# All of w_mod and wq read by rows behind the first K tile, the last wo rows read behind the last V tile, three unread products before the last layer

## The chip, the cores and the metric

One NeuronCore of a Trainium2 chip runs the whole program. The metric is the device time of one execution in microseconds (us). TensorE (PE) multiplies matrices into PSUM, VectorE (DVE) and ScalarE (ACT) do elementwise work, SyncE (SP) issues nearly all transfers (DMAs), which then run on 16 DMA engines in the order of issue. All data are 32-bit floats.

## The reference

A transformer block for one decoded token of 8 sequences, with adaptive layer norm:

```
mod = silu(c) @ w_mod                       # [8, 6*512], split into sa, ca, ga, sb, cb, gb
h = layernorm(x) * (1 + ca) + sa
q = h @ wq                                  # 32 heads of 128
p = softmax(q . k_cache[last 2048] / sqrt(128))   # 8 K/V heads, 4 query heads share one
x = x + ga * ((p . v_cache[last 2048]) @ wo)
h = layernorm(x) * (1 + cb) + sb
x = x + gb * (relu(h @ w1 + b1)**2 @ w2 + b2)
```

K and V of the window are 64 MiB each; w_mod is 6 MiB, wq and wo 8 MiB each, w1 and w2 3.5 MiB each.

## The kernel before, in words

**Buffers.** SBUF holds two "big" slots of 4 MiB and five "small" slots of 2 MiB (line 79). A K tile, which is half the batch of one K/V head, takes a big slot (16 of them, K0 to K15); a V tile, which is two sequences of one head, takes a small one (32, V0 to V31). Weights pass through the same slots.

**Order of the transfers.** One list, `loads` (lines 144 to 152), is the order in which SP issues every load; `pump` issues the next one as soon as a slot of its size is free in the program's order, and SP then waits until the slot's last reader is done. The list begins K0, columns of w_mod for sa and ca ("modA", 2 MiB), half of wq in two pieces, K1, the other half of wq, K2. Then comes a K tile followed by two V tiles, with a quarter of wo (2 MiB, a pair of heads) ahead of every eighth V tile: the last quarter stands ahead of V28. Behind V31 come the other four sixths of w_mod ("modB", 4 MiB, two DMAs), b1 and b2, w1 in two DMAs, w2 in four.

**Order of the compute.** It is written out by hand: PE executes in program order. The beginning makes mod's first two parts, the layer norm, and q (`project_q`, heads 0 to 3 first, 4 to 7 at step 4), with the first transposes of K0 in between. The main loop (line 501) has 38 steps, two steps to a K tile. A step transposes half a K tile on PE (line 231), which ACT and DVE copy out of PSUM (line 233), multiplies queries with it (line 359), and runs the V product `weighted` (line 451) five steps behind. A head's softmax (`soft_a` to `soft_d`), the gathering of its output (`gather`, line 475) and its product with wo (`project_o`, line 490) are placed at fixed steps. In step 33 stand, one behind the other, gather of head 6, the rest of head 7's softmax, the V product with V28, and `project_o(6)`; V29, V30 and V31 follow in steps 34 to 36, then in step 37 gather and `project_o(7)`.

**The end.** `at_i` copies the attention output out of PSUM (lines 540 and 541), `modulation` makes ga, sb, cb (line 543, 16 products of 384 columns) and gb (line 564, 16 of 128 columns), line 552 spreads at_i over partitions, x1 and its layer norm follow, then w1 (line 594), the squared ReLU (602 to 606), one product that nothing reads (line 611), w2 (line 614), and the output.

Of the kernel before, what the change touches and what calls it, by code (L numbers as in the profile page):

```python
# [20 lines left out]
def tile_adaln_cached_attention_mlp(  # L21
# [65 lines left out]
    def size_of(key):  # L87
        return "big" if key[0] in ("K", "modB") or key == ("wo", HKV // 2 - 1) else "small"

    def load(key):  # L90
        kind, i = key
        if kind == "b":
            nc.sync.dma_start(b1_in, b1.rearrange("(g n) -> g n", g=NQ))
            nc.sync.dma_start(b2_in, b2.rearrange("(g n) -> g n", g=NQ))
            return
        held[key] = free[size_of(key)].pop(0)
        t = slots[size_of(key)][held[key]]
        if kind in "KV":
# [7 lines left out]
            nc.sync.dma_start(t, v)  # L106
            return
        if kind == "wo":

            r = 2 * REP * DH  # L110
            v = wo[i * r : (i + 1) * r, :].rearrange("(h p i) n -> p h (i n)", p=P, i=4)
        elif kind == "modA":
            v = w_mod[:, : 2 * D].rearrange(r_kc, p=P)
        elif kind == "modB":
            v = w_mod.rearrange(r_kc, p=P)
            for lo, hi in ((2, 5), (5, 6)):
                nc.sync.dma_start(
                    t[:, NQ * D * (lo - 2) : NQ * D * (hi - 2)].rearrange("p (a n) -> p a n", a=NQ),
                    v[:, :, D * lo : D * hi],
                )  # L120
            return
        elif kind == "wq":
            r, half = divmod(i, 2)
            v = wq[:, 2048 * r : 2048 * r + 2048].rearrange(r_kc, p=P)[:, 2 * half : 2 * half + 2]
        elif kind == "w1":
            v = w1.rearrange(r_kc, p=P)[:, 2 * i : 2 * i + 2]
        else:
            v = w2.rearrange("(p c) n -> p c n", p=P)
            for lo, hi in ((0, 8),) if i == 0 else ((8, 12), (12, 13), (13, 14)):
                o = lo - 8 * i  # L130
                n = hi - lo
                nc.sync.dma_start(
                    t[:, D * o : D * (o + n)].rearrange("p (c n) -> p c n", n=D), v[:, lo:hi, :]
                )
            return
        a, n = v.shape[1:]
        nc.sync.dma_start(t[:, : a * n].rearrange("p (a n) -> p a n", n=n), v)

    def slot(key, n):

        t = slots[size_of(key)][held[key]]
# [18 lines left out]
    def done(*keys):  # L160
        for k in keys:
            free[size_of(k)].append(held.pop(k))
        pump()
# [58 lines left out]
    def transposes(q, g, e):  # L222

        k = slot(("K", q), DH)
        if e == 0:
            KTS[q, g] = ktp.tile([P, 4, 16, 32], F32, name="kT")
        t = KTS[q, g]
        for a in range(2):
            p = ps_kt.tile([P, 4, P], F32, name="kt_ps")
            for i in range(4):  # L230
                nc.tensor.transpose(p[:, i, :], k[:, 32 * e + 8 * g + 4 * a + i, :], ident)  # L231
# [21 lines left out]
    def modulation(wms, nq):  # L253

        pm = ps_m.tile([P, 512], F32, name="m_ps", tag="m_ps")
        for kc in range(NQ):
            wv = wms[kc].rearrange("p (m q n) -> p m q n", m=nq, q=NQ)
            for q in range(NQ):
                nc.tensor.matmul(
                    pm[32 * q : 32 * q + 32, : nq * P].rearrange("p (m n) -> p m n", m=nq),  # L260
                    cT[:, kc, :],
                    wv[:, :, q, :],
                    start=(kc == 0),
                    stop=(kc == NQ - 1),
                )
        return pm[:, : nq * P].rearrange("p (m n) -> p m n", m=nq)

# [8 lines left out]

    EARLY = [(0, 0), (0, 1), (0, 2)]
    transposes(0, 0, 0)
    transposes(0, 0, 1)
# [4 lines left out]
    modA = consts.tile([P, 2, P], F32, name="modA")  # L284
    m = slot(("modA", 0), 2 * D)
    pm = modulation([m[:, kc, :] for kc in range(NQ)], 2)
    done(("modA", 0))
    nc.vector.tensor_copy(modA[:, 0, :], pm[:, 0, :])
    nc.vector.tensor_scalar(modA[:, 1, :], pm[:, 1, :], 1.0, None, op0=ALU.add)
# [11 lines left out]
    h = work.tile([P, P], F32, name="h_sb", tag="one_h_sb", bufs=1)  # L301
    nc.vector.scalar_tensor_tensor(h, x_in, nmean, modA[:, 1, :], op0=ALU.add, op1=ALU.mult)
    transposes(0, 1, 0)
# [5 lines left out]
    nc.vector.scalar_tensor_tensor(h, h, rstd, modA[:, 0, :], op0=ALU.mult, op1=ALU.add)  # L309
    hT = consts.tile([P, NQ, 32], F32, name="h1T")  # L310
    to_columns(h, hT)
    transposes(0, 1, 1)

    def project_q(r, between=()):
        pq = ps_m.tile([P, 512], F32, name="m_ps", tag="m_ps")
        for kc in range(NQ):
            w = slot(("wq", 2 * r + kc // 2), 2048)
            for g in range(4):
                nc.tensor.matmul(  # L319
                    pq[32 * g : 32 * g + 32, :],  # L320
                    hT[:, kc, :],
                    w[:, kc % 2, 512 * g : 512 * g + 512],
                    start=(kc == 0),
                    stop=(kc == NQ - 1),
                )
            if kc % 2:
                done(("wq", 2 * r + kc // 2))
                if between:
                    transposes(*between[kc // 2])
        qs = work.tile([P, 512], F32, name="qs", tag="a", bufs=1)  # L330
        nc.scalar.copy(qs, pq)
# [8 lines left out]
    project_q(0, ((0, 2, 0), (0, 2, 1)))  # L340
# [101 lines left out]
    def weighted(n, h):  # L442
# [6 lines left out]
        for g in range(4):  # L449
            j = 8 * g + 4 * h  # L450
# [35 lines left out]
    def project_o(hk):  # L486

        w = slot(("wo", hk // 2), D)
# [8 lines left out]
        if hk % 2:  # L497
            done(("wo", hk // 2))


    for s in range(N + PV_LAG + 1):
# [4 lines left out]
        if s == C:  # L506
            project_q(1)
# [18 lines left out]
        if s < N:  # L526
            scores(q, 2 * h)
        if i == 0 and soft:
            soft_b(g - 1)
# [12 lines left out]
    m = slot(("modB", 0), 3 * D)  # L542
    pm = modulation([m[:, kc, :] for kc in range(NQ)], 3)
    ga = consts.tile([P, P], F32, name="ga")
    mul = consts.tile([P, P], F32, name="mul")
    add = consts.tile([P, P], F32, name="add")
    nc.scalar.copy(ga, pm[:, 0, :])
    nc.vector.tensor_scalar(mul, pm[:, 2, :], 1.0, lo, op0=ALU.add, op1=ALU.mult)
    nc.vector.tensor_scalar(add, pm[:, 1, :], hi, None, op0=ALU.mult)
# [13 lines left out]
    m = slot(("modB", 0), D)  # L563
    pmC = modulation([m[:, 3 * NQ + kc, :] for kc in range(NQ)], 1)
# [11 lines left out]
    modC = consts.tile([P, P], F32, name="modC")  # L576
    nc.scalar.copy(modC, pmC[:, 0, :])
# [3 lines left out]
    w1t = [slot(("w1", k), F) for k in range(2)]  # L581
    w2t = [slot(("w2", k), D) for k in range(2)]
# [28 lines left out]
    nc.tensor.matmul(spin_ps, ident, ident[:, None, :].to_broadcast([P, 4, P]), start=True, stop=True)  # L611
    for f in range(FC):
        for q in range(NQ):
# [3 lines left out]
                w2t[f // 8][:, f % 8, q * P : (q + 1) * P],  # L617
# [43 lines left out]
```

## Time and profile before

| | |
|---|---|
| median of 3 runs | 397.95 us (397.9 to 398.24) |
| the profiled execution | 399.03 us |
| its span, first to last instruction | 397.2 us |
| PE busy | 327.0 us, 82% of the span |
| DVE, ACT busy | 179.1 us, 97.0 us |
| moved by DMA | 165.22 MB, mean 416 GB/s |
| mean granted PE clock | 0.974 |

The profile is of one execution. Its views used below: the page (busy shares in 40 equal slices; queues), the timeline (each row: start, duration, engine, line, what it writes and reads, how often; in brackets how long the engine had been idle and what ended that), the DMA view (us from issue to landing) and windows (busy time of each engine in a stretch, then the granted PE clock, the busy share of the DMA engines, GB/s). Durations on PE are modelled: rows of one engine overlap a little.

### The profile page before, as it was taken

The numbers are of one execution on the slowest core, as the hardware profiler recorded it, in microseconds if no ns is written. First come the engines' busy times: TensorE is split into PE (matmuls) and PEld (weight loads), VectorE is DVE, ScalarE is ACT, GpSimd is POOL, SyncE is SP. The second block draws the span as 40 slices with busy tenths as digits, with TensorE's granted clock in tenths as the row PEclk, the third lists the DMA queues.
The fourth block names the chain that finished last, engine by engine and source line by source line (L and its number), as shares of the span: only waits on it lengthen the run. The fifth ranks groups of instructions, "written<-read, shape, count | busy, mean of one in ns | idle before, by whom it ended". The sixth has DMA issues, their size and how long they took to land.

```text
span 397.2 us, 6042 instructions
## 1 busy us (share of the span) xinstructions
PE 327.0 (82%) x2574; PEld 165.4 (42%) x2574; DVE 179.1 (45%) x417; ACT 97.0 (24%) x169; POOL 2.4 (1%) x12
## 2 busy tenths in 40 slices
PE   0477979796989968999869898998978789979574
PEld 0343535443444534444434444544444344533134
DVE  6142323553454435545623455555535364456320
ACT  1132224221222213123212232223122222230010
POOL 2000000000000000000000000000000000000000
PEclk9999999999899989999998999999999899989998
DMA  8999999999999999999999999999999999999992
GB/s 333 408 439 411 435 426 449 404 445 407 437 429 427 442 416 444 410 441 412 447 412 447 409 440 421 436 412 439 424 434 431 424 427 419 426 431 410 421 415 97
DMA packets 11867, 165.22 MB, mean 416 GB/s; under 512 B 1080, under 2 KB 1344, under 8 KB 3136
## 3 DMA queue, kind: packets, MB, share of 16 engines
q1 hardware_dynamic: 11696, 164.71, 97.7%
q8 instruction: 20, 0.33, 0.3%
q10 hardware_dynamic: 144, 0.13, 0.1%
q14 instruction: 7, 0.06, 0.0%
HBM read 164.77 MB, written 0.07 MB: 415 GB/s over the span
## 4 chain that ended last, share of the span: by engine, by line
DMA 44%; PE 41%; DVE 9%; ACT 4%; issue 1%; SPq 0%; ACTq 0%; DVEq 0%
DMA big<-in_A_k_cache_dram 33%; PE kt_ps L231 17%; PE s_ps L359 9%; PE o_ps L451 9%; DMA small<-in_B_w_dram 6%; DMA small<-in_w_mod_dram 4%; ACT pr L403 2%; DVE o_sb L467 2%; PE m_ps L475 2%; DVE kT L233 2%; DVE tr L479 1%; PE m_ps L614 1%; DVE pT L430 1%; PE m_ps L319 1%; PE m_ps L436 1%
## 5 line engine op out<-in xcount | busy, mean ns | idle before, releaser
L231 PE MATMUL kt_ps<-ident,big 128*128 128x128 f32 x1024 | 146.1, 286 | 45.9 <-DMA big<-in_A_k_cache_dram 35.8
L231 PEld LDWEIGHTS kt_ps<-ident,big 128*128 128x128 f32 x1024 | 113.0, 144 | 143.2 <-ACT kT L233 76.3
L233 DVE COPY kT<-kt_ps 128x512 f32<-128x512 f32 x128 | 88.3, 690 | 142.3 <-PE kt_ps L231 142.3
L233 ACT COPY kT<-kt_ps 128x512 f32<-128x512 f32 x128 | 74.8, 584 | 220.7 <-PE kt_ps L231 216.5
L359 PE MATMUL s_ps<-kT,qwin 128*32 128x512 f32 x512 | 71.5, 633 | 0.8 <-DVE qwin L345 0.8
L451 PE MATMUL o_ps<-small,pT 128*32 128x512 f32 x512 | 67.3, 603 | 0.1
L467 DVE SCALAR_TENSOR_TENSOR o_sb<-o_ps,diag,o_sb 128x128 f32<-128x128 f32 x96 | 33.7, 351 | 3.4
L465 DVE TENSOR_SCALAR o_sb<-o_ps,diag 128x128 f32<-128x128 f32 x32 | 11.2, 351 | 12.8 <-PE o_ps L451 12.8
L451 PEld LDWEIGHTS o_ps<-small,pT 128*32 128x32 f32 x512 | 11.1, 108 | 13.1 <-issue 11.6
L359 PEld LDWEIGHTS s_ps<-kT,qwin 128*32 128x32 f32 x512 | 10.4, 110 | 13.1 <-issue 11.4
L403 ACT ACTIVATE pr<-ss,nm 128x512 f32<-128x512 f32 x8 | 9.7, 1219 | 19.1 <-DVE nm L400 19.1
L427 PE MATMUL m_ps<-ident,pr 128*128 128x128 f32 x64 | 10.3, 289 | 2.2 <-DVE tr L479 2.2
L475 PE MATMUL m_ps<-o_sb,pick 128*128 128x512 f32 x16 | 9.3, 666 | 3.1 <-DVE o_sb L467 1.6
L427 PEld LDWEIGHTS m_ps<-ident,pr 128*128 128x128 f32 x64 | 7.7, 147 | 8.4 <-DVE tr L479 4.0
L430 DVE TENSOR_TENSOR pT<-m_ps,mine 128x512 f32<-128x512 f32 x16 | 10.4, 685 | 0.0
L371 DVE TENSOR_REDUCE mx<-ss 128x1 f32<-128x512 f32 x8 | 5.5, 687 | 8.6 <-ACT ss L369 8.5
L411 DVE COPY pr<-pr 128x512 f32<-128x512 f32 x8 | 3.4, 429 | 12.1 <-ACT pr L403 12.1
L319 PE MATMUL m_ps<-small,h1T 128*32 128x512 f32 x64 | 7.5, 597 | 1.5 <-DVE h1T L242 1.5
L369 ACT COPY ss<-s_ps 128x512 f32<-128x512 f32 x8 | 4.7, 587 | 11.5 <-PE s_ps L359 11.5
L479 DVE STREAM_TRANSPOSE tr<-m_ps 128x512 f32<-128x512 f32 x8 | 5.7, 717 | 2.5 <-PE m_ps L475 2.5
L614 PE MATMUL m_ps<-small,rT 128*32 128x128 f32 x112 | 4.8, 349 | 1.8 <-DMA small<-in_B_w_dram 1.8
L490 PE MATMUL wo_ps<-small,oT 128*32 128x512 f32 x48 | 6.2, 592 | 0.0
(124 smaller groups left out, 93.7 us busy)
## 6 DMA issues: line engine op xcount, KB each, us to landing
big<-in_A_k_cache_dram SPq DMA_DIRECT2D x16, 4096.0 KB, 23.6
small<-in_A_v_cache_dram SPq DMA_DIRECT2D x32, 2048.0 KB, 25.9
small<-in_A_wq_dram SPq DMA_DIRECT2D x4, 2048.0 KB, 35.4
small<-in_A_wo_dram SPq DMA_DIRECT2D x3, 2048.0 KB, 23.9
small<-in_B_w_dram SPq DMA_DIRECT2D x2, 1792.0 KB, 20.8
big<-in_w_mod_dram SPq DMA_DIRECT2D x1, 3072.0 KB, 22.5
small<-in_w_mod_dram SPq DMA_DIRECT2D x1, 2048.0 KB, 17.2
big<-in_A_wo_dram SPq DMA_DIRECT2D x1, 2048.0 KB
```

What stands on the lines that cost most here:

```text
L231: nc.tensor.transpose(p[:, i, :], k[:, 32 * e + 8 * g + 4 * a + i, :], ident)
L233: (nc.vector.tensor_copy if a else nc.scalar.copy)(t[:, :, i : i + 4, :], p.rearrange("p i (r u) -> p u i r", u=4))
L319: nc.tensor.matmul(pq[32 * g : 32 * g + 32, :], hT[:, kc, :], w[:, kc % 2, 512 * g : 512 * g + 512], start=(kc == 0), stop=(kc == NQ - 1),)
L359: nc.tensor.matmul(s_ps[0][32 * u : 32 * u + 32, :], qwin[hk % 2][:, 4 * c + u, o : o + 32], kT[:, u].rearrange("p i r -> p (i r)"), start ...
L403: nc.scalar.activation(pr.rearrange("p i (r e) u -> p e i r u", e=2)[:, :, :, :, 0], SS_.pop(hk).rearrange("p (e i r) -> p e i r", e=2, i= ...
L427: nc.tensor.transpose(pp[:, i * P : (i + 1) * P], pr[:, 4 * a + i].rearrange("p r u -> p (r u)"), ident)
L430: nc.vector.tensor_mul(PT_[hk][:, a].rearrange("p x i r -> p i x r"), pp.rearrange("p (i x r) -> p i x r", i=4, r=2 * REP), mine.rearrange ...
L451: nc.tensor.matmul(o[32 * g : 32 * g + 32].rearrange("p j d -> p (j d)"), PT_[hk][:, h, 4 * c + g].rearrange("p i r -> p (i r)"), v[:, j : ...
L465: nc.vector.tensor_scalar(d, o[:, 0, :], diag[:, 0:1], None, op0=ALU.mult)
L467: nc.vector.scalar_tensor_tensor(d, o[:, j, :], diag[:, j : j + 1], d, op0=ALU.mult, op1=ALU.add)
L475: nc.tensor.matmul(pp, pick.rearrange("p t u -> p (t u)"), o.rearrange("p c d -> p (c d)"), start=True, stop=True)
L479: nc.vector.transpose(tr, pp.rearrange("p (c d i) -> p c i d", c=C, i=4))
```

## The change

**Loads.** w_mod is no longer read by columns in two parts, but whole, in four DMAs, one for each kc: of the rows `4p + kc` one goes to partition p, 12 KiB in a piece (before: pieces of 4, 6 and 2 KiB). wq is read the same way, in four DMAs with pieces of 16 KiB (before 8 KiB). All eight stand behind K0 and ahead of K1. V0 moves ahead of K2. The last quarter of wo no longer stands ahead of V28: it is the first half of a new load "tail", behind V31, whose second half is half of w1. Then come the rest of w1 and w2, now in one big slot. A clause splits the V tile with the key `("V", N * 2 - 1)` into two DMAs.

**Compute.** One loop makes all six parts of mod at the beginning, in two PSUM tiles, row by row as they land, with the transposes of K0 in between; ga, mul, add and modC are kept until the end, where both calls of `modulation` are gone. q is made for all 8 heads at once; only its transposition (`turn_q`) is split. The tokens of K and V are taken in another order inside a tile (the same on both sides of the softmax). The unread product at the end stands three times.

```
-        return "big" if key[0] in ("K", "modB") or key == ("wo", HKV // 2 - 1) else "small"
+        return "big" if key[0] in ("K", "tail", "w2") else "small"
...
-            nc.sync.dma_start(t, v)
+            for x in range(2 if key == ("V", N * 2 - 1) else 1):
+                cols = slice(x * NJ * DH // 2, (x + 1) * NJ * DH // 2) if key == ("V", N * 2 - 1) else slice(None)
+                nc.sync.dma_start(t[:, cols], v[..., cols])
...
+        elif kind == "mod":
+            rows(0, w_mod.rearrange(r_kc, p=P)[:, i : i + 1])
         elif kind == "wq":
...
+            rows(0, wq.rearrange(r_kc, p=P)[:, i : i + 1])
+        elif kind == "tail":
+            rows(0, wo_rows(HKV // 2 - 1))
+            rows(NJ * DH, w1v[:, 0:2])
         elif kind == "w1":
...
+            rows(0, w1v[:, 2:4])
...
-    loads = [("K", 0), ("modA", 0), ("wq", 0), ("wq", 1), ("K", 1), ("wq", 2), ("wq", 3), ("K", 2)]
+    loads = [("K", 0), *(("mod", k) for k in range(NQ)), *(("wq", k) for k in range(NQ)), ("K", 1), ("V", 0), ("K", 2)]
...
-            if v % (2 * C) == 2 * C - 4:
+            if v % (2 * C) == 2 * C - 4 and v < 6 * C:
                 loads.append(("wo", v // (2 * C)))
-            loads.append(("V", v))
-    loads += [("modB", 0), ("b", 0), ("w1", 0), ("w1", 1), ("w2", 0), ("w2", 1)]
+            if v:
+                loads.append(("V", v))
+    loads += [("b", 0), ("tail", 0), ("w1", 0), ("w2", 0)]
...
+    pms = [ps_m.tile([P, 512], F32, name="m_ps", tag="m_ps") for _ in range(2)]
+    for kc in range(NQ):
+        if kc < 3:
+            transposes(0, kc, 0)
+            transposes(0, kc, 1)
+        wv = slot(("mod", kc), 6 * D)[:, 0].rearrange("p (m q n) -> p m q n", m=6, q=NQ)
+        for pm, m0, m1 in zip(pms, (0, 4), (4, 6)):
+            for q in range(NQ):
...
+        done(("mod", kc))
...
     def project_o(hk):
 
-        w = slot(("wo", hk // 2), D)
+        last = hk // 2 == HKV // 2 - 1
+        w = slot(("tail", 0) if last else ("wo", hk // 2), D)
...
-    pm = modulation([m[:, kc, :] for kc in range(NQ)], 3)
...
-    pmC = modulation([m[:, 3 * NQ + kc, :] for kc in range(NQ)], 1)
...
-    nc.tensor.matmul(spin_ps, ident, ident[:, None, :].to_broadcast([P, 4, P]), start=True, stop=True)
+    for _ in range(3):
+        nc.tensor.matmul(spin_ps, ident, ident[:, None, :].to_broadcast([P, 4, P]), start=True, stop=True)
```

**Where instructions stand.** On SP, the last loads before the change, from K15 (`big1<-in_A_k_cache`) on; "waits" names the semaphores an issue waits for (DMAHW: an earlier transfer's, PE: a reader of the slot):

```order
L106 DMA big1_92<-in_A_k_cache_dram 128x1x8192 [waits DMAHW4_49,PE_49]
L106 DMA small2_95<-in_A_v_cache_dram 128x1x4096 [waits DMAHW5_49,PE_49]
L106 DMA small3_96<-in_A_v_cache_dram 128x1x4096 [waits DMAHW6_49,PE_49]
L137 DMA big0_91<-in_A_wo_dram 128x2x2048 [waits DMAHW7_49,PE_49]
L106 DMA small0_93<-in_A_v_cache_dram 128x1x4096 [waits DMAHW0_49,PE_49]
L106 DMA small4_97<-in_A_v_cache_dram 128x1x4096 [waits PE_49]
L106 DMA small1_94<-in_A_v_cache_dram 128x1x4096 [waits DMAHW1_49,PE_49]
L106 DMA small2_95<-in_A_v_cache_dram 128x1x4096 [waits DMAHW3_49,PE_49]
L117 DMA big1_92<-in_w_mod_dram 128x4x1536 [waits DMAHW2_49]
L117 DMA big1_92<-in_w_mod_dram 128x4x512
```

The same stretch of SP in the changed kernel, from K15 to the first half of w1:

```order
L108 DMA big1_92<-in_A_k_cache_dram 128x1x8192 [waits DMAHW7_49,PE_49]
L108 DMA small0_93<-in_A_v_cache_dram 128x1x4096 [waits DMAHW0_49,PE_49]
L108 DMA small1_94<-in_A_v_cache_dram 128x1x4096 [waits DMAHW1_49,PE_49]
L108 DMA small3_96<-in_A_v_cache_dram 128x1x4096 [waits DMAHW3_49,PE_49]
L108 DMA small2_95<-in_A_v_cache_dram 128x1x4096 [waits PE_49]
L108 DMA small4_97<-in_A_v_cache_dram 128x1x4096 [waits DMAHW4_49,DMAHW2_49,PE_49]
L108 DMA small0_93<-in_A_v_cache_dram 128x1x4096 [waits DMAHW6_49,PE_49]
L93 DMA b1_in_80<-in_B_b1_dram 4x448
L94 DMA b2_in_81<-in_B_b2_dram 4x128 [waits DMAHW5_49]
L113 DMA big0_91<-in_A_wo_dram 128x2x2048
L113 DMA big0_91<-in_B_w1_dram 128x3584 [waits DMAHW7_49]
```

The wo rows stood third behind K15 and now stand behind the sixth and last V tile (V31, one DMA of 4096 numbers a partition in both) and the two small bias loads; w_mod is gone from here.

On PE, from `project_o(6)` in step 33 to the first product behind the loop, before the change (`wo_ps<-big0`: project_o; o_ps: the V products with V29, V30, V31; `m_ps<-o_sb`: gather; L259: modulation):

```order
L490 MATMUL wo_ps_114<-big0_91,oT0_136 32x512 [waits DMAHW5_49]
L490 MATMUL wo_ps_114<-big0_91,oT0_136 32x512 x3
L451 MATMUL o_ps_2931<-small4_97,pT_2895 32x512 [waits DMAHW7_49]
L451 MATMUL o_ps_2931<-small4_97,pT_2895 32x512 x7
L451 MATMUL o_ps_2945<-small1_94,pT_2895 32x512 [waits DMAHW0_49,DVE_49,PE_49]
L451 MATMUL o_ps_2945<-small1_94,pT_2895 32x512 x7
L451 MATMUL o_ps_2961<-small2_95,pT_2895 32x512 [waits DMAHW1_49,DVE_49,PE_49]
L451 MATMUL o_ps_2961<-small2_95,pT_2895 32x512 x7
L475 MATMUL m_ps_2974<-o_sb_2922,pick_131 128x512 [waits DVE_49]
L490 MATMUL wo_ps_114<-big0_91,oT1_137 32x512 [waits DVE_49]
L490 MATMUL wo_ps_114<-big0_91,oT1_137 32x512 x3
L259 MATMUL m_ps_2987<-big1_92,cT_151 32x384 [waits DMAHW2_49]
```

The same stretch of PE in the changed kernel:

```order
L488 MATMUL wo_ps_113<-big0_91,oT0_135 32x512 [waits DMAHW6_49]
L488 MATMUL wo_ps_113<-big0_91,oT0_135 32x512 x3
L448 MATMUL o_ps_2959<-small2_95,pT_2924 32x512 [waits DMAHW1_49]
L448 MATMUL o_ps_2959<-small2_95,pT_2924 32x512 x7
L448 MATMUL o_ps_2972<-small4_97,pT_2924 32x512 [waits DMAHW2_49,DVE_49,PE_49]
L448 MATMUL o_ps_2972<-small4_97,pT_2924 32x512 x7
L448 MATMUL o_ps_2985<-small0_93,pT_2924 32x512 [waits DMAHW3_49,DVE_49,PE_49]
L448 MATMUL o_ps_2985<-small0_93,pT_2924 32x512 x7
L472 MATMUL m_ps_2998<-o_sb_2950,pick_130 128x512 [waits DVE_49]
L488 MATMUL wo_ps_113<-big0_91,oT1_136 32x512 [waits DVE_49]
L488 MATMUL wo_ps_113<-big0_91,oT1_136 32x512 x3
L545 MATMUL m_ps_3011<-at_i_3008,sel_104 32x128 [waits DVE_49]
```

The order on PE is the same as before up to the last `project_o`; `project_o(6)`, ahead of the V products with V29, V30 and V31, waits for the semaphore of the wo transfer in both. Behind `project_o(7)` the 16 products of `modulation` no longer stand ahead of line 545 (552 before).

More of the change, by code (lines that the diff above doesn't have):

```diff
@@ L251, in tile_adaln_cached_attention_mlp @@
     nc.vector.tensor_copy(cT[:, :, B : 2 * B], cT[:, :, :B])
[L253 to L266, printed above, removed]
     lo = consts.tile([P, 1], F32, name="lo")
@@ L275, in tile_adaln_cached_attention_mlp @@
     nc.vector.tensor_copy(bsel[:, :, B : 2 * B], ident[:NQ, :NQ, None].to_broadcast([NQ, NQ, B]))
-    EARLY = [(0, 0), (0, 1), (0, 2)]
-    transposes(0, 0, 0)
-    transposes(0, 0, 1)
+    EARLY = [(0, g) for g in range(4)]
     qsel = consts.tile([NQ, NQ, 32], F32, name="qsel")
     nc.vector.tensor_copy(qsel, ident[:NQ, :NQ, None].to_broadcast([NQ, NQ, 32]))
[L284 to L289, printed above, removed]
     xsum = work.tile([P, 1], F32, name="xsum")
@@ L325, in project_q, with turn_q @@
                 )
[L326 to L329, printed above, removed]
+        done(("mod", kc))
+    pm = [pms[m // 4][:, m % 4 * P : m % 4 * P + P] for m in range(6)]
+    ga, mul, add, modC = (consts.tile([P, P], F32, name=n) for n in ("ga", "mul", "add", "modC"))
+    nc.vector.scalar_tensor_tensor(h, pm[1], 1.0, h, op0=ALU.add, op1=ALU.mult)
+    nc.vector.tensor_add(h, h, pm[0])
+    hT = consts.tile([P, NQ, 32], F32, name="h1T")
+    to_columns(h, hT)
+    nc.scalar.copy(ga, pm[2])
+    nc.vector.tensor_scalar(add, pm[3], hi, None, op0=ALU.mult)
+    nc.vector.tensor_scalar(mul, pm[4], 1.0, lo, op0=ALU.add, op1=ALU.mult)
+    nc.scalar.copy(modC, pm[5])
+    pqs = [ps_m.tile([P, 512], F32, name="m_ps", tag="m_ps") for _ in range(2)]
+    for kc in range(NQ):
+        w = slot(("wq", kc), 512)
+        for r in range(2):
+            for g in range(4):
+                nc.tensor.matmul(
+                    pqs[r][32 * g : 32 * g + 32, :],
+                    hT[:, kc, :],
+                    w[:, 4 * r + g, :],
+                    start=(kc == 0),
+                    stop=(kc == NQ - 1),
+                )
+        done(("wq", kc))
+    def turn_q(r):
         qs = work.tile([P, 512], F32, name="qs", tag="a", bufs=1)
-        nc.scalar.copy(qs, pq)
+        nc.scalar.copy(qs, pqs[r])
         pT_ = ps_m.tile([P, 512], F32, name="m_ps", tag="m_ps")
@@ L496, in project_o @@
             )
-        if hk % 2:
+        if hk % 2 and not last:
             done(("wo", hk // 2))
@@ L527, in tile_adaln_cached_attention_mlp @@
             scores(q, 2 * h)
+        if s == 0:
+            transposes(0, 3, 0)
+            transposes(0, 3, 1)
         if i == 0 and soft:
```

84 lines of the change are left out of this document (25 added, 59 removed).

## Prediction

> **What bounds the kernel now.** I read the page first, then the transfers' rows, then the timeline from K14 to the end. From the page, the span, the busy share of the 16 DMA engines in 40 slices, and the main DMA queue:
>
> ```profile
> span 397.2 us, 6042 instructions
> DMA  8999999999999999999999999999999999999992
> q1 hardware_dynamic: 11696, 164.71, 97.7%
> ```
>
> The DMA engines are full from the first slice to the last but one, and one queue fills them for 97.7% of the span. So the time is that of one stream of 165 MB, plus what is left to do when its last bytes are in. PE still counts at the end, as the timeline shows. First, K13's and K14's first transposes:
>
> ```profile
> 290.58 1.06 PE L231 MATMUL kt_ps<-ident,big 128*128 128x128 f32 x8 [2.47 <-DMA big<-in_A_k_cache_dram]
> ...
> 310.07 1.59 PE L231 MATMUL kt_ps<-ident,big 128*128 128x128 f32 x8 [3.30 <-DMA big<-in_A_k_cache_dram]
> ```
>
> PE waits for K14 until 310.07. From there to the output, the timeline's rows that carry the sum:
>
> ```profile
> 360.89 1.04 PE L490 MATMUL wo_ps<-big,oT 128*32 128x512 f32 x8
> 361.75 5.68 PE L451 MATMUL o_ps<-small,pT 128*32 128x512 f32 x48
> 372.88 0.37 ACT L541 COPY at_i<-wo_ps 128x256 f32<-128x256 f32 x1 [15.00 <-DVE at_i L540]
> 375.56 0.40 PE L552 MATMUL m_ps<-at_i,sel 128*32 128x128 f32 x8
> 376.63 0.28 DVE L557 TENSOR_TENSOR x<-m_ps,ga 128x128 f32<-128x128 f32 x1
> 377.68 1.08 PE L259 MATMUL m_ps<-big,cT 128*32 128x128 f32 x32
> 378.39 0.42 DVE L242 STREAM_TRANSPOSE h2T<-xm 128x128 f32<-128x128 f32 x1
> 380.00 1.71 PE L594 MATMUL m_ps<-small,h2T 128*32 128x448 f32 x16 [0.30 <-DMA small<-in_B_w_dram]
> 381.64 0.39 PE L589 MATMUL m_ps<-ssb,ones 128*128 128x8 f32 x2
> 384.19 1.71 PE L594 MATMUL m_ps<-small,h2T 128*32 128x448 f32 x16 [2.16 <-DMA small<-in_B_w_dram]
> 385.83 0.48 PE L609 MATMUL m_ps<-b_in,qsel 4*128 4x128 f32 x2
> 385.97 0.65 DVE L242 STREAM_TRANSPOSE rc<-m_ps 128x448 f32<-128x448 f32 x1 [3.40 <-PE m_ps L594]
> 386.24 1.12 PE L611 MATMUL kt_ps<-ident 128*128 128x512 f32 x2
> 387.35 0.28 DVE L606 SCALAR_TENSOR_TENSOR rT<-relu 128x112 f32<-128x112 f32 x1
> 389.17 4.80 PE L614 MATMUL m_ps<-small,rT 128*32 128x128 f32 x112 [1.80 <-DMA small<-in_B_w_dram]
> 394.04 0.29 DVE L622 TENSOR_TENSOR y<-m_ps,modC 128x128 f32<-128x128 f32 x1 [6.42 <-PE m_ps L614]
> ```
>
> Line 594 waits twice, and line 614 once, for weights: the stream sets the end, with little to spare, for PE comes to line 594 when w1 has just landed (0.30). The stretch from 310.07 to there is PE's and its helpers' own.
>
> **The stream.** Its bytes stay the same, the pieces get longer. SP's issue rows, and from the DMA view (us from issue to landing last) V31, the two modB transfers, and at the start the first two behind K0:
>
> ```profile
> 1.44 0.58 SPq L137 DMA_DIRECT2D small<-in_w_mod_dram  x1
> 2.07 0.61 SPq L137 DMA_DIRECT2D small<-in_A_wq_dram  x1
> ...
> 349.84 0.54 SPq L106 DMA_DIRECT2D small<-in_A_v_cache_dram  x1
> 350.42 1.27 SPq L117 DMA_DIRECT2D big<-in_w_mod_dram  x2
> ```
>
> ```profile
> small<-in_w_mod_dram SPq DMA_DIRECT2D x1, 2048.0 KB, 17.2
> small<-in_A_wq_dram SPq DMA_DIRECT2D x1, 2048.0 KB, 21.6
> ```
>
> ```profile
> small<-in_A_v_cache_dram SPq DMA_DIRECT2D x1, 2048.0 KB, 15.5
> ```
>
> ```profile
> big<-in_w_mod_dram SPq DMA_DIRECT2D x1, 1024.0 KB, 24.5
> ```
>
> And from the windows, busy times, then PE's granted clock, DMA share and GB/s:
>
> ```profile
> 310.00:315.00 5.00, 4.93 (x28) 2.62 (x32) 1.48 (x3) 1.75 (x3) 0.00 (x0) 0.66 1.00 426
> 340.00:345.00 5.00, 5.00 (x43) 2.65 (x45) 2.92 (x7) 1.76 (x3) 0.00 (x0) 1.00 1.04 436
> 385.00:390.00 5.00, 3.20 (x33) 1.54 (x29) 1.48 (x4) 0.00 (x0) 0.00 (x0) 0.90 0.78 321
> 390.00:395.00 5.00, 3.97 (x103) 3.71 (x94) 0.58 (x2) 0.00 (x0) 0.00 (x0) 0.76 0.12 45
> ```
>
> V31 lands at 349.84 + 15.5 = 365.3. The second modB transfer is issued about 0.65 behind the first and lands at 351.1 + 24.5 = 375.6. So modB's 4.19 MB take 10.3 us of stream, 410 GB/s; a wq piece, 2.1 MB, takes 23.7 - 18.6 = 5.1 us. Where K and V pass in long pieces, at 426 to 436 GB/s, they would take 9.7 and 4.9. w_mod's new pieces are 12 KiB and wq's 16, nearer to those, but the two rates are of single stretches: I take 0.9 us of savings for all of w_mod and wq together, with 0 and 1.6 (0.6, and 5 times 0.2) as ends. By the Trainium skill (DMA: Bandwidth & Descriptors, Where 436 GB/s comes from) a load from HBM is bound at about 358 GB/s; modB would then take 11.7 us and all that follows it would come 1.4 us later, but the rows here run at 410 to 436, so the sum goes by these.
>
> **wo comes late: the step that decides.** All that stood ahead of the last wo piece still does, and V28 to V31 as well, and modB's 4 MiB. In the stream its place is therefore where modB's end was, less the savings: it lands at 375.6 - 0.9 = 374.7 (374.0 to 375.6). When does PE want it? K14 also has modB's bytes ahead of it now, so it lands 10.3 - 0.9 = 9.4 us later, at 319.4, and PE, idle for 3.30 us before it already, has nothing else to do. From there to `project_o(6)` its work is unchanged, 360.89 - 310.07 = 50.8 us. It comes there at 370.3, and waits 4.4 us for wo. Behind this wait stand, on PE, the V products with V29 to V31, the gather, `project_o(7)` and everything after; before, wo had been in long before 360.89. V29 to V31 are in SBUF by 370 (365.3 + 9.4 - 5, the wo piece being gone from ahead of them), so they cost nothing.
>
> **From there to the end.** The chain is counted in differences of the rows above, from the landing at 374.7.
> - `project_o(6)` to the end of at_i's copy: 373.25 - 360.89 = 12.4, to 387.1.
> - Clock: after 3.30 us of idle the products at 310.07 took 1.59 instead of 1.06, and the granted clock was 0.66 over 5 us, some 1.7 us lost. After 4.4 us of idle I add 1.5 (0 to 1.7): 388.6.
> - modulation's two calls are gone: their 2.79 + 1.08 us were partly cover for the late w1. Now line 552's 0.40 and a hand-over follow at_i (0.5), then lines 557 to 242, 378.81 - 376.63 = 2.2: 391.3.
> - w1 has landed, so line 594 runs without waits: 1.64 to line 589, 0.3, 1.64 again: 394.9.
> - The bias product 0.4 and three unread products instead of one: PE gives 512 columns in 0.86 (360.89 to 361.75 is the like, four at a time in quarters), 2.6 together: 397.9. The squares would be ready at 391.3 + 1.94 + 1.78 + 1.66 = 396.7, so the added products cost 1.2 here.
> - w2's products: 4.80 with the clock at 0.90 and 0.76; at full clock line 259 does 32 such in 1.08, so 112 take some 3.6 (3.4 to 4.8): 401.5. All of w2 landed by about 392.
> - From there to the span's end as before, 397.2 - 394.0 = 3.2: 404.7.
>
> That is 7.5 us more than 397.2. The windows of 385 to 395 show the clock at 0.90 and 0.76 after a gap of only 1.80 us on PE, so the unread products give back with a warm clock (4.8 to 3.6) what they cost. By the Trainium skill (TensorE: Matmul & The Clock Gate, Part 1) the clock falls only after an idle window of about 3.4 us; by that the products would cost their 1.2 for nothing, and the span without two of them would be 403.5. The windows say otherwise, and so I also leave room for a second cold stretch in the thin work behind at_i.
>
> **The other edits.** At the start, the timeline's rows for the first scores and for the issue of K2 that follows K0's last transposes:
>
> ```profile
> 33.74 1.92 PE L359 MATMUL s_ps<-kT,qwin 128*32 128x512 f32 x16 [0.76 <-DVE qwin L345]
> ...
> 38.73 0.55 SPq L106 DMA_DIRECT2D big<-in_A_k_cache_dram  x1
> ```
>
> The changed kernel makes mod with 32 products there instead of 16, and q for all heads, while 14.7 MB of w_mod and wq pass: 34.5 us at 426 GB/s, from 13.5 (18.6 - 5.1, K0's end) to 48. PE has nothing but K0 to work on in that time, so this is covered by the transfers. Only an empty stream would cost: K2 needs K0's slot. Turning q takes some 3 us, then scores and K0's last quarter some 5 (33.7 to 38.7), so K2 is issued near 56, while K1 and V0 keep the queue busy to 63 (6.3 MB more): 7 us of cover, less the 2 or so from issue to first byte. w2 as one big slot waits for K15's last transposes, 350.4 + 9.4, long before the stream gets to it. The other order of tokens, and ga to modC made early by ACT and DVE, which idle then, cost nothing.
>
> The halved V tile does not exist: the keys run to ("V", 31), the clause asks for 63, and SP's order shows V31 in one piece. In halves it would change nothing either, since PE waits for wo ahead of it.
>
> **The rivals.**
> 1. The stream sets the end, as before, and wo is no wait. Then w2's last piece lands 0.9 earlier and warm products save up to 1.2 more: span 395.1 to 396.3, time near 396.6, faster. For it speaks that line 614 waits for the stream now. It decides only if PE gets through step 33 so early that the squares are ready when w2's first piece lands, near 388: they come 12.4 + 0.5 + 2.2 + 1.94 + 1.78 + 1.66 = 20.5 behind `project_o(6)`, so that would have to start by 367.5, with wo in; PE alone is there at 370.3. 4%.
> 2. wo lands just before 370.3, so only K14's delay counts, without a cold clock: 370.3 + 12.4 + 0.5 + 2.2 + 3.6 + 3.0 + 3.6 + 3.2: span 398.8, time 399.6. It needs wo 4.4 us earlier than the rows give. 5%.
> 3. The queue also runs dry: V31's slot comes free only when V26's product is done, 359 by PE's 9.4 us of delay, and K2 and K3 wait on K0 and K1. Each us of an empty queue is a us later for wo: 1.5 to 3 us, time 407 to 408.5. Against it: K2 has some 5 us to spare by the count above, and V30, 4.9 us of stream, lands near 365, so most of it is still to come at 359. 9%.
>
> **How the numbers follow.** The forecast itself has 82%. The profiled execution is 399.03 with a span of 397.2; the median of the runs is 397.95, 1.1 less. I add the 7.5 to the median: 405.4. Its own range: wo -0.7 to +0.9, clock -1.5 to +0.2, w2 -0.2 to +1.2, a second cold stretch in the thin work after at_i up to +1: 403.0 to 407.5; with part of rival 3 and some of what PE gives back I say 402.5 to 408. A measurement of this kernel tells 0.2% (0.8 us) from no change. Rivals 2 and 3 and the forecast are slower by more than that, though rival 2 could fall within it (1 of its 5): slower 0.95. Rival 1 is split into faster 0.03 and same 0.01; same is 0.02 in all.
>
> **What would show it.** In the new profile PE's longest late wait should be `project_o(6)` for wo's transfer, some 4 us, near 374.7; line 604's products (w2) should start with all weights in, waiting for DVE or PE, near 398; the DMA share should be full until about 387 and the PE clock low just after 374. Wrong it is if wo's product does not wait, if K14 lands other than near 319, or if the chain from wo to the end is much under 29 us.

## The result and the profile after

The changed kernel takes 408.41 us, the median of four runs (407.58, 407.62, 409.21 and 410.61); the kernel before takes 397.94. The ratio is 1.027 (95% interval 1.0225 to 1.0315): slower, by 3.0 us more than the 405.4 forecast. Of all the runs reported here one, at 413.76 us, counts as slow (over 1.5% above the fastest of its kernel) and is left out of median and ratio. The profiled execution is the slowest of the four, 410.61 with a span of 408.8. From its page:

```profile
span 408.8 us, 5977 instructions
PE 339.2 (83%) x2546; PEld 166.1 (41%) x2546; DVE 178.8 (44%) x416; ACT 97.3 (24%) x169; POOL 2.4 (1%) x12
DMA  8999999999999999999999999999999999999910
q1 hardware_dynamic: 10176, 164.71, 94.8%
```

The same 164.71 MB now fill 94.8% of the span instead of 97.7%: the last two slices of the DMA row are nearly empty, where before only the last one was low. PE itself is busy for 339.2 us instead of 327.0, though the program has 65 instructions fewer. From the waits, in us in total, times, and the longest:

```profile
PE kt_ps L230 <- DMA big<-in_A_k_cache_dram: 16.4, 7, 3.5
PE wo_ps L488 <- DMA big<-in_A_wo_dram: 5.6, 1, 5.6
```

The second is new. From the timeline, V31's issue and wo's, then PE and its helpers from K14's first transposes to the output (line 230 transposes, 448 the V product, 488 `project_o`, 583 w1, 604 w2):

```profile
357.91 0.53 SPq L108 DMA_DIRECT2D small<-in_A_v_cache_dram  x1
...
359.38 0.40 SPq L113 DMA_DIRECT2D big<-in_A_wo_dram  x1
```

```profile
319.72 1.06 PE L230 MATMUL kt_ps<-ident,big 128*128 128x128 f32 x8 [1.74 <-DMA big<-in_A_k_cache_dram]
...
367.22 1.92 PE L448 MATMUL o_ps<-small,pT 128*32 128x512 f32 x16
374.74 1.94 PE L488 MATMUL wo_ps<-big,oT 128*32 128x512 f32 x8 [5.60 <-DMA big<-in_A_wo_dram]
376.45 7.24 PE L448 MATMUL o_ps<-small,pT 128*32 128x512 f32 x48
385.32 1.13 PE L472 MATMUL m_ps<-o_sb,pick 128*128 128x512 f32 x2 [1.62 <-DVE o_sb L464]
387.50 1.94 PE L488 MATMUL wo_ps<-big,oT 128*32 128x512 f32 x8 [1.05 <-DVE oT L477]
...
394.17 3.12 PE L583 MATMUL m_ps<-big,h2T 128*32 128x448 f32 x16
397.22 0.39 PE L578 MATMUL m_ps<-ssb,ones 128*128 128x8 f32 x2
397.54 1.71 PE L583 MATMUL m_ps<-small,h2T 128*32 128x448 f32 x16
399.18 0.48 PE L598 MATMUL m_ps<-b_in,qsel 4*128 4x128 f32 x2
399.59 2.84 PE L601 MATMUL kt_ps<-ident 128*128 128x512 f32 x6
402.37 3.26 PE L604 MATMUL m_ps<-big,rT 128*32 128x128 f32 x112
```

```profile
390.01 0.37 ACT L542 COPY at_i<-wo_ps 128x256 f32<-128x256 f32 x1 [24.05 <-DVE at_i L541]
...
405.70 0.29 DVE L612 TENSOR_TENSOR y<-m_ps,modC 128x128 f32<-128x128 f32 x1 [4.72 <-PE m_ps L604]
```

K14's transposes start at 319.72 instead of 310.07, the wait for wo ends at 374.74, and from there no product waits for a transfer. V31 is one DMA: the clause that halves a V tile does nothing. Three groups look alike in their shapes and differ in duration (the timeline counts each product twice, so that the four of line 488 stand as x8): the products of line 488 take 1.94 where before they took 1.04, the V products behind them 7.24 (before 5.68), and the first half of line 583 3.12, the second 1.71. The windows say why; the third number from the end is PE's granted clock:

```profile
370.00:375.00 5.00, 0.26 (x4) 0.20 (x8) 0.69 (x2) 0.00 (x0) 0.00 (x0) 0.82 1.02 429
375.00:380.00 5.00, 5.00 (x28) 1.12 (x24) 0.00 (x0) 0.00 (x0) 0.00 (x0) 0.50 1.02 435
380.00:385.00 5.00, 3.70 (x36) 0.79 (x28) 3.94 (x12) 0.00 (x0) 0.00 (x0) 1.00 0.99 422
385.00:390.00 5.00, 3.08 (x12) 0.52 (x12) 1.62 (x4) 0.00 (x0) 0.00 (x0) 0.68 0.72 291
390.00:395.00 5.00, 4.18 (x20) 1.63 (x24) 2.20 (x9) 0.87 (x3) 0.00 (x0) 0.50 0.06 19
395.00:400.00 5.00, 5.00 (x37) 1.62 (x30) 0.85 (x2) 0.27 (x1) 0.00 (x0) 0.79 0.00 0
```

The clock is half for a whole window twice. If it is always either full or half, as these two suggest, the first three rows hold 2 x 5 x (0.18 + 0.50) = 6.8 us of half clock and the last three 2 x 5 x (0.32 + 0.50 + 0.21) = 10.3.

### The profile page after: what moved, and what is told of

It is laid out like the page before. It is cut to its first block, busy times and chain, and to the rows that moved or that the text cites. A ratio compares the mean times of both kernels' runs of the same rounds, so it can differ in the third digit from the quotient of the medians.

```text
span 408.8 us, 5977 instructions
## 1 busy us (share of the span) xinstructions
PE 339.2 (83%) x2546; PEld 166.1 (41%) x2546; DVE 178.8 (44%) x416; ACT 97.3 (24%) x169; POOL 2.4 (1%) x12
## 3 DMA queue, kind: packets, MB, share of 16 engines
q1 hardware_dynamic: 10176, 164.71, 94.8%
## 4 chain that ended last, share of the span: by engine, by line
PE 56%; DMA 29%; DVE 8%; ACT 4%; issue 1%; SPq 0%; ACTq 0%; DVEq 0%
PE kt_ps L230 24%; DMA big<-in_A_k_cache_dram 20%; PE o_ps L448 11%; PE s_ps L356 11%; DMA small<-in_A_wq_dram 5%; DMA big<-in_A_wo_dram 4%; ACT pr L400 2%; DVE o_sb L464 2%; PE wo_ps L488 2%; PE m_ps L472 2%; DVE kT L232 2%; DVE tr L476 1%; PE m_ps L292 1%; ACT kT L232 1%; PE m_ps L583 1%
## 5 line engine op out<-in xcount | busy, mean ns | idle before, releaser
L356 PE MATMUL s_ps<-kT,qwin 128*32 128x512 f32 x512 | 70.3, 624 | 0.8 <-DVE qwin L342 0.8
L448 PE MATMUL o_ps<-small,pT 128*32 128x512 f32 x512 | 69.1, 619 | 0.0
L317 PE MATMUL m_ps<-small,h1T 128*32 128x512 f32 x64 | 11.5, 853 | 11.4 <-DMA small<-in_A_wq_dram 11.4
L356 PEld LDWEIGHTS s_ps<-kT,qwin 128*32 128x32 f32 x512 | 10.3, 109 | 12.8 <-issue 11.1
L317 PEld LDWEIGHTS m_ps<-small,h1T 128*32 128x32 f32 x64 | 2.2, 133 | 19.8 <-DMA small<-in_A_wq_dram 10.8
L488 PE MATMUL wo_ps<-big,oT 128*32 128x512 f32 x16 | 3.9, 1062 | 6.7 <-DMA big<-in_A_wo_dram 5.6
L292 PE MATMUL m_ps<-small,cT 128*32 128x512 f32 (+1 forms) x64 | 6.4, 521 | 1.4 <-DMA small<-in_w_mod_dram 1.4
```

The costliest lines, as they stand in the source:

```text
L292: nc.tensor.matmul(pm[32 * q : 32 * q + 32, : (m1 - m0) * P].rearrange("p (m n) -> p m n", n=P), cT[:, kc, :], wv[:, m0:m1, q, :], start=( ...
L317: nc.tensor.matmul(pqs[r][32 * g : 32 * g + 32, :], hT[:, kc, :], w[:, 4 * r + g, :], start=(kc == 0), stop=(kc == NQ - 1),)
L356: nc.tensor.matmul(s_ps[0][32 * u : 32 * u + 32, :], qwin[hk % 2][:, 4 * c + u, o : o + 32], kT[:, u].rearrange("p i r -> p (i r)"), start ...
L448: nc.tensor.matmul(o[32 * g : 32 * g + 32].rearrange("p j d -> p (j d)"), PT_[hk][:, h, 4 * c + g].rearrange("p i r -> p (i r)"), v[:, j : ...
L488: nc.tensor.matmul(wo_ps[32 * i : 32 * i + 32, :], oT[hk % 2][:, i, :], w[:, 4 * (hk % 2) + i, :], start=(hk == 0), stop=(hk == HKV - 1),)
```

## The experiments

Nine kernels were run. The theory: wo's late landing makes PE wait, K14's delay has made PE late already, and in the tail PE runs at half clock, since waits and thin work follow each other there. The rivals: wo's place costs little or nothing (something else made the kernel slower), and the clock is only a small correction. The kernel before took 398.08 us (median) beside the first four, 398.38 beside the next four, 398.47 beside the last. The changed kernel was not run again beside them, so a difference from its 408.41 is one between sets, and sure to some 0.5 us only.

**wo's rows ahead of V28 again**, everything else as changed. The half of w1 that shares wo's slot ("w1a" here) keeps its place behind V31:

```
...
-            if v % (2 * C) == 2 * C - 4 and v < 6 * C:
-                loads.append(("wo", v // (2 * C)))
+            if v % (2 * C) == 2 * C - 4:
+                loads.append(("wo", v // (2 * C)) if v < 6 * C else ("tail", 0))
...
-    loads += [("b", 0), ("tail", 0), ("w1", 0), ("w2", 0)]
+    loads += [("b", 0), ("w1a", 0), ("w1", 0), ("w2", 0)]
...
```

> The changed kernel with one thing undone: the last wo piece is loaded ahead of V28 again, everything else as changed. Theory A (wo behind V31 makes project_o(6) wait, and the wait cools PE's clock): no wait for wo; V31 now lands at 374.7 instead of 369.75 and is waited for, about 1 us, the chain behind it is 21 us and 3.2: span 398 to 400, time 400 to 402, 6 to 8 us under the changed kernel, still 2 to 4 over the kernel before, because K14 is 9.6 us late. Theory B (w_mod whole at the start makes K14 late and that alone sets the end): within 1 us of the changed kernel, 407 to 409.

It took 403.81 us (403.18 to 404.64; ratio 1.0142, 1.0123 to 1.016). From its timeline:

```profile
368.80 1.04 PE L492 MATMUL wo_ps<-big,oT 128*32 128x512 f32 x8
369.66 3.62 PE L452 MATMUL o_ps<-small,pT 128*32 128x512 f32 x32
374.99 1.92 PE L452 MATMUL o_ps<-small,pT 128*32 128x512 f32 x16 [1.71 <-DVE o_sb L468]
...
387.39 3.11 PE L587 MATMUL m_ps<-big,h2T 128*32 128x448 f32 x16
```

`project_o` does not wait, so wo's place is worth 4.6 us, and the rival that it is worth nothing (407 to 409) falls. But the time is nearly 2 above the upper end expected: V31's product waits in wo's stead until 374.99 (V31, issued at 357.75, lands 17.1 later, at 374.85; the profile names DVE for the wait, but the 48 rows of V products above run on without waiting for it), and w1's first half (line 587 here) is again slow, 3.11.

**`project_o(6)` behind V31's product**, with the changed kernel's loads:

```
+        if v == N:
+            project_o(HKV - 2)
...
-        if v >= C and v % C == 0:
+        if v >= C and v % C == 0 and v != N - C:
             project_o(v // C - 1)
```

> The changed kernel's loads, but on PE project_o(6) stands behind the V product with V31 instead of ahead of the one with V29. Theory A: PE goes on with V29 to V31 while wo comes, wo's product waits under 1 us near 374.7, span 396 to 398, time 398 to 400. If the wait only moves and what follows is as late as before (a rival: the chain behind wo's landing is what counts, wherever V29 to V31 stand): 374.7 + 28 and more, 406 to 408.

It took 400.43 us (399.34 to 402.01; ratio 1.0058, 1.0032 to 1.0084), just above the range. From its timeline:

```profile
367.98 7.25 PE L448 MATMUL o_ps<-small,pT 128*32 128x512 f32 x64
375.01 1.07 PE L488 MATMUL wo_ps<-big,oT 128*32 128x512 f32 x8
```

The V products, with V28 to V31 in 7.25 us, fill the time in which wo lands. With wo's load as late as in the changed kernel, moving one product on PE takes off 8.0 us, more than moving the load back. So it is the idle PE that costs, not the late load as such; that its span, 398.6, is close to the 398.8 that rival 2 of the prediction gave for K14's delay alone is chance, for that rival had wo in by 370.3, and here its product runs at 375.01.

**Six unread products ahead of `project_o(6)`**, to keep PE busy while it waits for wo:

```
+        if v == N - C:
+            idle = ps_kt.tile([P, 4, P], F32, name="kt_ps")
+            for _ in range(6):
+                nc.tensor.matmul(idle, ident, ident[:, None, :].to_broadcast([P, 4, P]), start=True, stop=True)
```

> The changed kernel with six products that nothing reads put ahead of project_o(6), 5.2 us of PE work inside its wait for wo, so that the clock stays up. Theory A with the clock as the mis-sized term: the first 6.8 us at half clock go, 2.5 to 3.4 us less, time 404 to 406 (if the second cold stretch, behind at_i, stays). If the clock were not the reason: no gain, 407.5 to 409.

It took 407.37 us (three runs, 406.1 to 410.15, without the one at 413.76; ratio 1.0242, 1.0194 to 1.0291): not the gain expected. It lies between the two expectations, and its runs overlap the changed kernel's, so that 1 us of gain cannot be told from none. From its timeline:

```profile
371.26 5.42 PE L538 MATMUL kt_ps<-ident 128*128 128x512 f32 x12
376.61 1.07 PE L488 MATMUL wo_ps<-big,oT 128*32 128x512 f32 x8
377.49 5.50 PE L448 MATMUL o_ps<-small,pT 128*32 128x512 f32 x48
...
393.35 3.21 PE L587 MATMUL m_ps<-big,h2T 128*32 128x448 f32 x16
```

The products behind the wait became fast, 1.07 and 5.50, but PE came to this place 2 us later in this run (V28's product at 369.41 for 367.22), the unread ones ran on until 376.6, and w1's first half stayed slow (3.21). The kernel shows that keeping PE busy mends the first stretch, and not what that is worth.

**Unread products in all of the tail's gaps**: four in wo's wait, one ahead of the last gather, one ahead of the last `project_o`, and a half one on either side of the products that spread at_i. `keep(n)` issues n of them, 512 columns each:

```
...
+        if v == N:
+            keep(1)
         if v >= C and v % C == 0:
             gather(v // C - 1)
...
+        if v == N - C:
+            keep(4)
+        if v == N:
+            keep(1)
         if v >= C and v % C == 0:
             project_o(v // C - 1)
...
```

> The changed kernel with products that nothing reads put into PE's idle times from project_o(6) to the last layer norm (four in the wait for wo, one ahead of the last gather, one ahead of project_o(7), two halves behind it), so that the clock stays up through the thin work; the transfers and the rest of the order are as changed. If the half clock is the term that was sized too small: the 4 us that the span had over the forecast go, time 404.5 to 406. If the products only stand in the way: 408 to 410.

It took 405.43 us (404.04 to 406.46; ratio 1.0178, 1.0147 to 1.0209), inside the range, with a profiled span of 403.0 in a run of 404.76. All its runs lie below all of the changed kernel's. From its windows and its timeline:

```profile
375.00:380.00 5.00, 5.00 (x48) 1.38 (x44) 2.02 (x6) 0.00 (x0) 0.00 (x0) 1.00 1.00 427
380.00:385.00 5.00, 4.24 (x22) 1.16 (x15) 3.12 (x9) 0.00 (x0) 0.00 (x0) 1.00 1.02 428
385.00:390.00 5.00, 4.62 (x28) 1.76 (x32) 2.54 (x10) 0.86 (x3) 0.00 (x0) 1.00 0.71 283
390.00:395.00 5.00, 5.00 (x39) 1.95 (x32) 1.56 (x5) 0.27 (x1) 0.00 (x0) 1.00 0.05 17
```

```profile
374.78 1.07 PE L488 MATMUL wo_ps<-big,oT 128*32 128x512 f32 x8
375.67 5.50 PE L448 MATMUL o_ps<-small,pT 128*32 128x512 f32 x48
...
389.73 1.71 PE L601 MATMUL m_ps<-big,h2T 128*32 128x448 f32 x16 [0.16 <-DVE h2T L241]
```

From the same start to 0.04 us, and with more products on PE, w1 starts 4.4 us earlier than in the changed kernel's profile (389.73 for 394.17), and the median is 3.0 lower. Nothing reads the added products: apart from the time they take, the clock is what they change, and the rows bear it out: `project_o(6)` and the V products behind it alone are 0.87 and 1.74 shorter than in the changed kernel. The forecast chain without any cold clock, 404.7 less its 1.5, gives 403.2 for this span.

**wo ahead, and unread products in the gaps** (two ahead of V31's product instead of four in wo's wait, the others as in the last):

```
...
+        if v == N - 1:
+            keep(2)
         if 0 <= v < N:
             weighted(v, 0)
...
```

> The changed kernel with wo's last rows ahead of V28 again, as in the run with wo ahead (403.81), and with unread products in the places where PE waits behind that: two full ones ahead of V31's product, one ahead of the last gather, one ahead of the last project_o, two halves around line 559. No product of the block is added, dropped or changed. Theory (what is left when wo waits for nothing is K14's delay, which makes V31 late, plus a low clock in the thin tail): in the run with unread products in the tail, V31's product ended at 381.1 and the span was 403.0, 21.9 later; here V31 lands near 374.9 and its product ends at 376.9 to 377.3, so the span is 398.8 to 399.5 and the time 400 to 401.5, 2 to 4 under the run with wo ahead though PE has more to do. Rival (the low clock cost nothing there; the added products only add): 404 or more.

It took 401.46 us (400.61 to 403.26; ratio 1.0093, 1.0064 to 1.0121), as expected, with full clock from 365 to 395. The rows that answer to those of the run with wo ahead:

```profile
375.07 1.92 PE L452 MATMUL o_ps<-small,pT 128*32 128x512 f32 x16
...
385.56 1.71 PE L605 MATMUL m_ps<-big,h2T 128*32 128x448 f32 x16 [0.15 <-DVE h2T L245]
```

V31's product starts at the same time, w1 1.8 us earlier. So the 10.5 us can be taken apart: 4.6 for wo's place (with what the clock costs behind the wait for wo), 2.3 for the clock in the rest of the tail (403.81 to 401.46; one of its four runs reaches into the other's), and 3.0 to 3.5 that are left (over the 398.47 beside this run, or over 397.94), with nothing waiting for wo and a full clock. That rest is not K14's delay as such: about 1.3 of it by the next run are the two added unread products, and the last kernel below, with K14 as late, is level with the kernel before.

**One unread product instead of three** in the changed kernel (`for _ in range(1)`):

> The changed kernel with one unread product ahead of w2's products, as before the change, instead of three. By the forecast two of them cost 1.2 to 1.5 us there, and what they give back (a warm clock for w2's products) is 1.2 to 1.5: same, 407.5 to 409. If they only cost: 406 to 407. If they are worth more than they cost: over 409.

It took 408.91 us (405.56 to 410.52; ratio 1.0257, 1.0208 to 1.0307): with a spread of 5 us the times cannot tell 1 us. **Three instead of one** in the kernel before:

> The kernel before with one edit: three unread products ahead of w2's products instead of one. They fit into PE's 1.8 us wait for w2 and keep the clock up; w2's products take 3.4 instead of 4.8 us but the last w2 piece lands near 392.8, so the end comes 0.5 to 0.8 us earlier: time 397.2 to 397.6. If the unread products are what slows the changed kernel: 399 or more.

It took 398.06 us, beside 398.38 (ratio 1.0008, 0.999 to 1.0026): the same, and not the gain of 0.5 to 0.8 expected. Its w2 products are fast, and wait for their last weights:

```profile
388.84 1.96 PE L615 MATMUL m_ps<-small,rT 128*32 128x128 f32 x64
391.20 1.71 PE L615 MATMUL m_ps<-small,rT 128*32 128x128 f32 x48 [0.41 <-DMA small<-in_B_w_dram]
```

The unread products keep the clock there, but the stream then sets the end. In the changed kernel the profile with one product has w2 start at 400.92, 1.45 earlier than with three (1.3, counted from the bias product ahead of them, 399.07 for 399.18), at the same 3.27 us: by these two profiles the two added products cost about 1.3 and gave nothing back. That profile also shows the same two stretches of half clock, 0.50 from 375 to 380, then 0.69, 0.50 and 0.79 from 385 to 400.

**Only wo's place changed, in the kernel before:**

```
-            if v % (2 * C) == 2 * C - 4:
+            if v % (2 * C) == 2 * C - 4 and v < 6 * C:
                 loads.append(("wo", v // (2 * C)))
...
-    loads += [("modB", 0), ("b", 0), ("w1", 0), ("w1", 1), ("w2", 0), ("w2", 1)]
+    loads += [("wo", HKV // 2 - 1), ("modB", 0), ("b", 0), ("w1", 0), ("w1", 1), ("w2", 0), ("w2", 1)]
```

> The kernel before with one edit: the last wo piece is loaded behind V31 instead of ahead of V28; w_mod and wq stay as before. Theory A, with the clock as it showed in the changed kernel: wo lands at 365.4, project_o(6) waits 4.5 us for it from 360.9, the first 7 us behind it run at half clock, and modulation stands behind it: time 400 to 402.5. A rival, that the stream still hides it because modB and w1 come as before: 398 to 399.

It took 399.31 us (397.97 to 401.86; ratio 1.0034, 1.0007 to 1.0062), between the two expectations. From its timeline:

```profile
365.03 1.93 PE L490 MATMUL wo_ps<-big,oT 128*32 128x512 f32 x8 [5.13 <-DMA big<-in_A_wo_dram]
...
390.08 3.27 PE L614 MATMUL m_ps<-small,rT 128*32 128x128 f32 x112 [0.31 <-DVE rT L606]
```

The wait for wo is as long as in the changed kernel (5.13 and 5.60), yet wo's late place costs 0.9 us there, in the median, and 4.6 here. With K14 on time, PE has the slack to wait: w2's products start only 0.9 us later than in the profile of before (390.08 for 389.17). But the 0.9 stands for no single run: the ten runs lie in two groups, five from 397.97 to 398.4, which is no loss, and five from 400.22 to 401.86, 1.8 to 3.5 over 398.38; the profile is of the first, and what parts the second was not seen.

**Both mended**: `project_o(6)` behind V31, one unread product at the end, and unread ones in the gaps of the tail.

> The changed loads with project_o(6) behind the V product with V31, one unread product ahead of w2 instead of three, and products that nothing reads in the idle times behind project_o(6). Theory A: 400.4 less 1.4 for the two products and 0.5 to 1.7 for the clock: 397.3 to 398.5, level with the kernel before, since K14 stays 9.6 us late and the stream ends near 391.5.

It took 398.6 us (397.54 to 401.49; ratio 1.0012, 0.9992 to 1.0031), level with the kernel before, in its expected range but for 0.1. K14's first transposes, w1's first half, and two of the windows:

```profile
320.41 1.06 PE L230 MATMUL kt_ps<-ident,big 128*128 128x128 f32 x8 [1.72 <-DMA big<-in_A_k_cache_dram]
...
383.36 2.87 PE L599 MATMUL m_ps<-big,h2T 128*32 128x448 f32 x16 [0.15 <-DVE h2T L241]
```

```profile
380.00:385.00 5.00, 4.62 (x28) 1.74 (x30) 2.27 (x10) 0.87 (x3) 0.00 (x0) 0.88 0.99 416
385.00:390.00 5.00, 5.00 (x30) 1.53 (x22) 1.40 (x4) 0.27 (x1) 0.00 (x0) 0.78 0.77 312
```

K14 is as late as in the changed kernel, and all the other edits are in. So the changed loads, with these three edits, need not cost anything, and here they bring nothing either. The unread products did not keep the clock full in this profile: it was half for 2 x 5 x (0.12 + 0.22) = 3.4 us. The kernel with wo ahead and products in the gaps is 2.9 slower, though K14 is no later there (319.86). It has two unread products more, and V31 lands last there: its product stands ahead of the last gather, which starts at 378.62. Here wo's product comes last, the gather does not need it, and starts at 376.42.

## Why the prediction was right in kind and short in size

**Right.** The deciding step held: wo landed in time for a start at 374.74 (forecast 374.7), K14's transposes started at 319.72 (319.4), PE waited 5.60 (4.4) because it came at 367.22 + 1.92 = 369.1, earlier than the 370.3 forecast. The stream set the end no more, w1 and w2 waited for nothing, and the start cost nothing that shows at K14. None of rivals 1 to 3 occurred; for the third, the DMA row shows no slice under 9 between the first and the stream's end. As forecast, no V tile is halved.

**Where it failed.** The step is the one on the clock: "After 4.4 us of idle I add 1.5 (0 to 1.7)", with "a second cold stretch in the thin work after at_i up to +1" kept only for the range. From wo's landing on, forecast against trace:

| stretch | forecast | measured | difference |
|---|---|---|---|
| `project_o(6)` to the end of at_i | 13.9 | 390.01 + 0.37 - 374.74 = 15.6 | +1.7 |
| to w1's first product | 2.7 | 3.8 | +1.1 |
| w1 | 3.6 | 5.0 | +1.4 |
| bias and three unread products | 3.0 | 3.2 | +0.2 |
| w2 | 3.6 | 3.3 | -0.3 |
| the end | 3.2 | 3.1 | -0.1 |

The sum is +4.0, which takes the forecast span of 404.7 to the 408.8 measured in the slowest of the four runs. The first three rows are those in which the windows show half clock, 17 us of it in two stretches, where the forecast had one of some 3. The kernel with products in all the gaps, whose clock is full from 375 on, came out at 403.0, near the forecast chain without its 1.5. So the wait and the chain were right, and the clock was the term that was sized too small. I had read the lesson from a place where the clock recovered: K14's first transposes, followed by dense work. Behind `project_o(6)` each hand-over to DVE leaves PE another gap. The modulation products that the change took away, 2.79 and 1.08 us, had been PE's work just there, and I had counted them as cover for w1's load only. Whether they kept the clock up is not shown: no run puts them back alone, and in the kernel before with three unread products the first of them ran partly at half clock themselves (3.89 us instead of 2.79, in windows of 0.50 and 0.85).

**The range.** The upper ends that I listed, 0.9 for wo, 0.2 for the clock, 1.2 for w2 and 1 for the second cold stretch, add up to 408.7 and not to the 407.5 written, so that 408.41 lies within the sum. That would be luck: wo landed when forecast and w2 took less than forecast, while in the profiled run the clock took more than its 0.2 and 1.

**The unread products.** I had them give back with a warm clock what they cost. They do keep a clock warm in the kernel before; in the changed one w2's products were at 3.27 with one as with three, for in both profiles the half clock ends at about 397, before them.

**From span to median.** I took the profiled execution of before, 1.1 above its median, as typical of the offset, and so added span differences to the median. The changed kernel's profiled execution is 2.2 above its own, and its runs spread over 3.0 us, where those beside it of before spread over 0.3 (over 0.9 to 1.4 in the later sets). A run's time is 1.8 to 1.9 over its span, so a span of 404.7 means 406.5: of the 3.0 us by which the median was missed, 1.1 are this step and 1.9 the chain. The spans of the runs go from 405.7 to 408.8: even the shortest is above the forecast's 404.7, so the miss is not only one of conversion.

**What stays open.** The 3.0 to 3.5 us that remain with wo early and the clock full were only left over, and beyond the 1.3 for the unread products they were not taken apart; no run moved K14 alone. When exactly the clock falls was not settled. What spreads the changed kernel's runs is open too: only one run of each kernel has a trace, and the mean clocks do not follow the spans (0.946, 0.962, 0.957 and 0.957 for 408.8, 407.3, 405.7 and 405.7).

## What to carry to other kernels

When a load is moved behind others, look at what PE could do in its wait: moving one instruction that needs the load behind those that don't took off 8.0 us, more than moving the load back. The price of a wait depends on which chain has slack: loading wo late, with the same 5 us wait, cost 0.9 us in the median where the stream set the end and 4.6 where PE did. Of two late loads, put last the one with the shorter chain behind it (400.43 us with wo last, 403.81 with V31 last, though part of that is the clock). Work taken out of a thin tail may have been what kept the clock up, so count the gaps that it leaves before booking its duration as a gain.

## What the runs showed of the hardware

The half clock does not need a long wait. In the changed kernel it held for some 10.3 us around 387 to 397, where PE's gaps were 1.62, 1.05, 0.55 and 0.82 us and PE was busy for 3.08 and 4.18 of 5 us in the first two windows. With wo ahead, where PE's longest gap from 370 on was 1.71, it held as long, 2 x 5 x (0.50 + 0.50 + 0.03) = 10.3:

```profile
375.00:380.00 5.00, 3.03 (x18) 0.75 (x18) 1.71 (x5) 0.00 (x0) 0.00 (x0) 1.00 1.02 431
380.00:385.00 5.00, 3.03 (x16) 0.57 (x16) 1.64 (x6) 0.37 (x1) 0.00 (x0) 0.50 0.99 421
385.00:390.00 5.00, 4.89 (x20) 1.59 (x20) 1.61 (x6) 0.49 (x2) 0.00 (x0) 0.50 0.72 288
390.00:395.00 5.00, 5.00 (x29) 2.06 (x26) 1.68 (x5) 0.27 (x1) 0.00 (x0) 0.97 0.06 20
```

The Trainium skill (TensorE: Matmul & The Clock Gate, HAM oscillation) warns of idle gaps over about 3.4 us; the first stretch, behind a wait of 5.60, agrees with that, the second came without such a gap. Part 1 of that page of the Trainium skill has a free-running activity window of about that length; the stretches of 3.4 us (with both mended), 6.8 and 10.3 us are close to one, two and three times 3.4, which fits it.

Unread products that brought the busy time to 4.24 to 5.00 us in each 5 us kept the clock full in the same stretch, and with wo ahead 4.42 to 5.00 did. With both mended it fell, though PE was busy for 4.04, 4.62 and 5.00 us of the three windows from 375 to 390. So busy time by itself gave no threshold here.
